# A fused hash-attention and gated-FFT kernel: whole-pair DMAs, transposes of two tokens of one head, bucket bits by DMA, weight split on GpSimd

## The chip, the cores and the metric

The kernel runs on one core of a Trainium2 chip. The metric is device time in microseconds (us): the median of several executions. Engines are called PE (TensorE matmul), VectorE or DVE, ScalarE or ACT, GpSimd or POOL, and SyncE or SP, which only issues DMAs here. A core has 16 DMA engines. Each engine works through its own instructions strictly in order. "Granted clock" is the TensorE clock that the throttle allowed, 1.0 being full speed.

## The reference, cut to what matters

Four batches, eight heads, 768 tokens, head size 64. Attention is masked by a hash: a query sees only the keys whose six projection signs ("bucket bits") equal its own. The result (512 wide) goes through three projections, a circular convolution of one of them along the tokens, a product of the three, and an output projection.

```python
q_bits = (np.einsum('bhsd,dk->bhsk', q, proj) > 0)       # proj: 64 x 6; k_bits likewise
mask = q_bucket[:, :, :, None] == k_bucket[:, :, None, :]
attn = softmax(where(mask, q @ k.T / 8, -1e9));  x = attn @ v        # per head
proj = x @ w_proj                                          # 512 -> 3 x 512: x1, x2, x3
x2_conv = irfft(rfft(x2) * rfft(filter))                   # along the 768 tokens
out = (x1 * x2_conv * x3) @ w_out
```

## The kernel before

The work goes by head pairs, 16 in all (four per batch). For a pair g the kernel loads q, k and v, transposes q and k on PE, copies them from PSUM to `tz` (DVE), casts them into the operands `row` (POOL), projects for the bits (`zps`, PE), and writes the bits beside q and k, so that one score matmul (`stp`) also carries the mask. ACT takes the exponential. `pv` multiplies with v; DVE makes T from it. Then the rows are normalised: the row sums travel to DRAM as reciprocals (`rdr`) and come back broadcast over partitions as R, and DVE multiplies: U = T * R. `xh` and `xl` are U split into two half-precision parts, the input of the projections (`x2`, `x`), which start when a batch's four pairs are done and run between the attention work of later pairs. The weights are split the same way once, early in the run.

The parts that matter (cuts marked `...`):

```python
def finish(g):                                   # end of a pair
    ...
    nc.vector.reciprocal(rl, rl)
    rdr = drp.tile([2, SEQ], FP32, ...)          # in DRAM; SEQ = 768
    nc.sync.dma_start(rdr.rearrange("h (p c) -> p h c", p=P), rl)
    R = nrm.tile([P, SEQ], FP32, tag="R", name="R", bufs=1)
    for par in range(2):                         # one DMA per head: 64 partitions each
        nc.sync.dma_start(
            R[HD * par : HD * par + HD, :], rdr[par : par + 1, :].to_broadcast([HD, SEQ])
        )
    ...
    nc.vector.scalar_tensor_tensor(              # U waits for R
        U, in0=T[:, 0:SEQ], scalar=vsd, op0=ALU.add, in1=R, op1=ALU.mult)
    nc.vector.tensor_copy(th, U)                 # xh
    nc.gpsimd.tensor_tensor(tl, U, th, ALU.subtract)   # xl

# loads of q and k: four DMAs each, runs of 256 bytes
for par in range(2):
    head = src[b, 2 * pr + par].rearrange("(c p j) d -> p c j d", c=3, p=P, j=2)
    ...
    for j in range(2):
        eng.dma_start(t_[:, :, j, par, :], head[:, :, j, :])

# bits: eight small DVE operations per pair
nc.vector.tensor_scalar(row[(which, par)][r0 : r0 + 6, cs], zs[hf][z0 : z0 + 6, :],
                        0.0, 0.5, ALU.is_gt, ALU.subtract)

# weight split, shared between DVE and POOL
nc.vector.tensor_copy(th, w32)
(nc.vector if c % 2 else nc.gpsimd).tensor_tensor(tl, w32, th, ALU.subtract)
```

The softmax here doesn't subtract the row's maximum and nothing guards it: scores larger than these inputs give would overflow.

## Time and profile before

| | before |
|---|---|
| time, median | 523.1 us (522.0 to 524.1) |
| PE busy / DVE / POOL | 469.4 / 322.5 / 156.1 us of 521.2 |
| projections start (first x2 matmul) | 113.7 us |
| first score matmul | 17.2 us |

The windows view of the kernel before, cut at the start of the projections: microseconds busy (instructions), granted clock, DMA share, GB/s.

```profile
core 0: us, PE busy (x) PEld busy (x) DVE busy (x) ACT busy (x) POOL busy (x), PEclk, DMA share, GB/s
0.00:113.70 113.70, 84.63 (x417) 40.99 (x418) 90.21 (x147) 61.62 (x81) 72.46 (x98) 0.91 0.63 162
113.70:521.20 407.50, 384.74 (x2137) 207.61 (x2135) 232.27 (x445) 168.20 (x241) 83.65 (x109) 0.99 0.19 53
```

PE's waits in the first 121 us of the kernel before (us in total, times, longest):

```profile
PE tps_q L198 <- DVE T L276: 6.6, 2, 5.2
PE tps_q L198 <- DMA nat_q<-in_q_dram: 4.6, 1, 4.6
...
PE hps L449 <- DVE pr_k_1_96 L232: 2.2, 1, 2.2
```

Apart from the first load, PE there waits for DVE's evacuations and bit writes.

### The profile page before, as it was taken

To read this page: it belongs to the slowest core of one execution; us is meant where nothing else is said; L and a number is where in the kernel's file an instruction comes from. 1 tells how busy PE (TensorE), PEld (TensorE's weight loads), DVE (VectorE), ACT (ScalarE), POOL (GpSimd) and SP (SyncE) were. 2 spreads that over 40 slices of the span, in tenths; PEclk is the share of its full clock that TensorE was granted. 3 is DMA by queue.
4 is the path that set the end of the run, shared out by engine and by line. 5 is a ranking of instruction groups with operands and counts; after the bars stand their busy time and mean duration, and the time that the engine had idled before them with its cause. 6 is when DMAs were issued, how large, how long until landed. Compare 5 with 4: busy or idle time off the path is not lost.

```text
span 521.2 us, 7013 instructions
## 1 busy us (share of the span) xinstructions
PE 469.4 (90%) x2552; PEld 248.6 (48%) x2552; DVE 322.5 (62%) x591; ACT 229.8 (44%) x321; POOL 156.1 (30%) x206
## 2 busy tenths in 40 slices
PE   4797657988998989999898998989999999999997
PEld 2343323544464545645354554645455556445553
DVE  4888987893756887353747878463645783036830
ACT  0496604883454553446365355336577310201102
POOL 4574993562414222232324131232311110000000
PEclk9898869998998999999999999999999999999999
DMA  9798514541313031324113040313010100300003
GB/s 215 186 287 218 171 32 102 123 121 34 91 32 91 1 93 32 93 91 139 45 32 91 14 109 1 93 44 120 20 32 1 33 30 1 121 1 1 0 2 121
DMA packets 82084, 39.93 MB, mean 77 GB/s; under 512 B 61953, under 2 KB 74753, under 8 KB 82049
## 3 DMA queue, kind: packets, MB, share of 16 engines
q1 hardware_dynamic: 78544, 38.62, 27.8%
q10 hardware_dynamic: 3504, 0.86, 0.8%
q8 instruction: 20, 0.33, 0.3%
q14 instruction: 16, 0.12, 0.1%
HBM read 32.97 MB, written 6.39 MB: 76 GB/s over the span
## 4 chain that ended last, share of the span: by engine, by line
PE 50%; DMA 17%; DVE 16%; issue 7%; POOL 5%; SPq 3%; ACT 2%; DVEq 0%; ACTq 0%; POOLq 0%
PE wout L488 8%; DMA R<-rdr 7%; PE pv L270 5%; DMA rdr<-rl 5%; PE stp L354 4%; PE x2b L488 3%; PE x2c L488 3%; PE zps L215 3%; PE x2a L488 2%; PE idrq L488 2%; DMA nat_v<-in_v_dram 2%; SPq L177 2%; PE fdft L488 2%; DVE U L304 1%; DMA flt_572<-in_moe_filter_fft_dram 1%
## 5 line engine op out<-in xcount | busy, mean ns | idle before, releaser
L276 DVE SCALAR_TENSOR_TENSOR T<-S,cst_sb,pv 64x512 f32<-64x512 f32 x64 | 38.9, 608 | 58.0 <-ACT S L275 57.3
L310 POOL TENSOR_TENSOR xl<-U,xh 128x768 f16<-128x768 f32 x16 | 26.5, 1654 | 97.0 <-DVE xh L308 97.0
L275 ACT COPY S<-pv 64x512 f32<-64x512 f32 x64 | 30.5, 477 | 46.1 <-PE pv L270 30.4
L215 PE MATMUL zps<-tz,projpad 128*38 128x384 f32 x128 | 29.0, 561 | 8.1 <-DVE tz L202 5.6
L198 PE MATMUL tps_q<-cst_sb,nat_q 128*128 128x128 f32 x96 | 24.9, 297 | 11.1 <-DVE T L276 6.6
L632 ACT ACTIVATE osb<-wout 128x512 f32<-128x512 f32 x24 | 14.3, 595 | 45.0 <-PE wout L488 44.9
L198 PE MATMUL tps_k<-cst_sb,nat_k 128*128 128x128 f32 x96 | 24.7, 288 | 7.7 <-DMA nat_k<-in_k_dram 2.5
L304 DVE SCALAR_TENSOR_TENSOR U<-T,vsd,R 128x768 f32<-128x768 f32 x16 | 16.5, 1032 | 23.5 <-DMA R<-rdr 20.5
L202 DVE TENSOR_SCALAR tz<-tps_q 128x384 f32<-128x384 f32 x32 | 17.6, 554 | 18.9 <-PE tps_q L198 18.4
L488 PEld LDWEIGHTS <-xh 128*128 128x128 f16 x192 | 18.9, 99 | 19.8 <-DVE xh L308 1.6
L198 PEld LDWEIGHTS tps_q<-cst_sb,nat_q 128*128 128x128 f32 x96 | 13.8, 151 | 20.4 <-DVE T L276 7.4
L359 ACT ACTIVATE pt_115<-stp,nmatch 128x768 f16<-128x768 f32 x16 | 14.5, 904 | 16.8 <-PE stp L354 16.6
L359 ACT ACTIVATE pt_111<-stp,nmatch 128x768 f16<-128x768 f32 x16 | 14.4, 901 | 15.5 <-PE stp L354 15.5
L198 PEld LDWEIGHTS tps_k<-cst_sb,nat_k 128*128 128x128 f32 x96 | 13.4, 147 | 16.4 <-issue 4.3
L359 ACT ACTIVATE pt_112<-stp,nmatch 128x768 f16<-128x768 f32 x16 | 14.4, 903 | 15.4 <-PE stp L354 15.2
L202 DVE TENSOR_SCALAR tz<-tps_k 128x384 f32<-128x384 f32 x32 | 17.5, 549 | 6.0 <-PE tps_k L198 4.0
L359 ACT ACTIVATE pt_106<-stp,nmatch 128x768 f16<-128x768 f32 x16 | 14.4, 902 | 14.9 <-PE stp L354 14.9
L359 ACT ACTIVATE pt_104<-stp,nmatch 128x768 f16<-128x768 f32 x16 | 14.4, 901 | 14.2 <-PE stp L354 7.3
L359 ACT ACTIVATE pt_110<-stp,nmatch 128x768 f16<-128x768 f32 x16 | 14.4, 902 | 11.8 <-PE pv L270 6.3
L354 PE MATMUL stp<-pr_q_0_87,pr_k_0_90 128*128 128x512 f16 x72 | 17.9, 325 | 1.6 <-ACT pt_108 L359 1.4
L354 PE MATMUL stp<-pr_q_0_86,pr_k_0_89 70*128 70x512 f16 x72 | 17.6, 333 | 1.7 <-ACT pt_104 L359 0.7
L488 PEld LDWEIGHTS <-wph_594 128*128 128x128 f16 x128 | 12.3, 98 | 13.8 <-issue 4.8
(1290 smaller groups left out, 1382.8 us busy)
## 6 DMA issues: line engine op xcount, KB each, us to landing
nat_q<-in_q_dram SPq DMA_DIRECT2D x64, 96.0 KB, 2.9
nat_v<-in_v_dram SPq DMA_DIRECT2D x32, 192.0 KB, 3.8
R<-rdr SPq DMA_DIRECT2D x32, 192.0 KB, 3.6
out_dram<-osb SPq DMA_DIRECT2D x24, 256.0 KB, 2.0
nat_k<-in_k_dram SPq DMA_DIRECT2D x56, 96.0 KB, 2.6
o_616<-in_moe_w_out_dram SPq DMA_DIRECT2D x1, 1024.0 KB, 7.5
nat_k<-in_k_dram ACTq DMA_DIRECT2D x8, 96.0 KB, 4.1
flt_572<-in_moe_filter_fft_dram SPq DMA_DIRECT2D x1, 768.0 KB, 7.1
```

Of the source, the lines that this page charges most:

```text
L198: nc.tensor.transpose(tps[:, ts(i, P)], nat[:, c3, j].rearrange("p h d -> p (h d)"), ident)
L202: nc.vector.tensor_scalar(tz[:, cs], tps, scl, None, ALU.mult)
L215: mm = nc.tensor.matmul(zps[64 * i : 64 * i + 38, :], projpad, tzs[i][:, cs])
L270: nc.tensor.matmul(pv, vpr[:, jt, :], pl[jt][:, lo_c:hi_c], start=(jt == 0), stop=(jt == NCH - 1),)
L275: nc.scalar.copy(S[rows, lo_c:hi_c], pv[HD:P, :])
L276: nc.vector.scalar_tensor_tensor(T[rows, lo_c:hi_c], in0=S[rows, lo_c:hi_c], scalar=mask[rows, :], op0=ALU.mult, in1=pv[0:HD, :], op1=ALU.add,
L304: nc.vector.scalar_tensor_tensor(U, in0=T[:, 0:SEQ], scalar=vsd, op0=ALU.add, in1=R, op1=ALU.mult)
L310: nc.gpsimd.tensor_tensor(tl, U, th, ALU.subtract)
L354: nc.tensor.matmul(stp[:, lo_c:hi_c], kp[kr, ts(jt, P)], qp[kr, lo_c:hi_c])
L359: nc.scalar.activation(pt[:, 0:SEQ], stp, AF.Exp, bias=nmatch, scale=LSCALE)
L488: nc.tensor.matmul(dest, lh, rh, start=(i == 0), stop=(i == len(terms) - 1))
L632: nc.scalar.mul(osb, po, 1.0 / YSCALE)
```

## The change

The intent: fewer and larger DMAs (q, k, v of a pair and R in one each, runs of 512 bytes), less DVE work (bits in two operations per pair and eight small DMAs; weight split on POOL). The transposed blocks now hold two tokens of one head instead of one token of two heads; the token order is carried through to the output. The core of the diff (cuts marked `...`; reorderings of v, of the convolution's output and of the stores, and the move of a few early loads to other DMA queues, are left out):

```diff
-    NPT = 12
+    NPT = 11
...
-        for par in range(2):
-            head = src[b, 2 * pr + par].rearrange("(c p j) d -> p c j d", c=3, p=P, j=2)
-            ... (one DMA for v, two for q and k, per head)
+        t_ = natp.tile([P, NCH, P], FP32, tag="nat", name=f"nat_{which}")
+        eng.dma_start(
+            t_,
+            src[b, 2 * pr : 2 * pr + 2].rearrange("h (c p j) d -> p (h c) (j d)", c=3, p=P, j=2),
+        )
...
-                for par, r0 in ((0, 64), (1, 0)):
-                    z0 = 64 * i + 32 * par
-                    nc.vector.tensor_scalar(
-                        row[(which, par)][r0 : r0 + 6, cs], zs[hf][z0 : z0 + 6, :],
-                        0.0, 0.5, ALU.is_gt, ALU.subtract,
-                    )
+            nc.vector.tensor_scalar(bt[:, par], zps, 0.0, 0.5, ALU.is_gt, ALU.subtract)
+            r0 = (64, 0)[par]
+            for i, which in enumerate(("q", "k")):
+                for j in range(2):
+                    z0 = HD * i + 6 * j
+                    nc.sync.dma_start(
+                        row[(which, par)][r0 : r0 + 6, HALF * j : HALF * j + HALF],
+                        bt[z0 : z0 + 6, par],
+                    )
...
-        for par in range(2):
-            nc.sync.dma_start(
-                R[HD * par : HD * par + HD, :], rdr[par : par + 1, :].to_broadcast([HD, SEQ])
-            )
+        rda = rdr[:, :]
+        nc.sync.dma_start(
+            R, bass.AP(tensor=rda.tensor, offset=rda.offset, ap=[[SEQ, 2], [0, HD], [1, SEQ]])
+        )
...
-            nc.vector.tensor_copy(th, w32)
+            nc.gpsimd.tensor_copy(th, w32)
...
-            (nc.vector if c % 2 else nc.gpsimd).tensor_tensor(tl, w32, th, ALU.subtract)
+            nc.gpsimd.tensor_tensor(tl, w32, th, ALU.subtract)
...
-            nc.vector.tensor_copy(th2, o32[:, c, :])
+            nc.gpsimd.tensor_copy(th2, o32[:, c, :])
```

More of the change, by code (lines that the diff above doesn't have):

```diff
@@ L134 @@
     cst_sb = cp.tile([P, P + 4], FP32, name="cst_sb")
-    nc.scalar.dma_start(cst_sb, cst_d.ap())
+    nc.scalar.dma_start(cst_sb[:, 0:P], cst_d.ap()[:, 0:P])
     ident = cst_sb[:, 0:P]
     mask = cst_sb[:, P : P + 1]
-    projpad = cp.tile([P, 38], FP32, name="projpad")
+    projpad = cp.tile([P, HD], FP32, name="projpad")
     nc.vector.memset(projpad, 0.0)
-    nc.scalar.dma_start(projpad[0:HD, 0:6], proj)
-    nc.scalar.dma_start(projpad[HD:P, 32:38], proj)
+    nc.gpsimd.dma_start(projpad[0:HD, 0:6], proj)
+    nc.gpsimd.dma_start(projpad[HD:P, 6:12], proj)
+    nc.gpsimd.dma_start(cst_sb[:, P : P + 4], cst_d.ap()[:, P : P + 4])
     nmatch = cp.tile([P, 1], FP32, name="nmatch")
@@ L167, in nat_load @@
     def nat_load(src, b, pr, which, eng):
-        shape = [P, 2, 3, 2, HD] if which == "v" else [P, 3, 2, 2, HD]
-        t_ = natp.tile(shape, FP32, tag="nat", name=f"nat_{which}")
-        for par in range(2):
-            head = src[b, 2 * pr + par].rearrange("(c p j) d -> p c j d", c=3, p=P, j=2)
-            if which == "v":
-                eng.dma_start(t_[:, par], head)
-            else:
-                for j in range(2):
-                    eng.dma_start(t_[:, :, j, par, :], head[:, :, j, :])
+        t_ = natp.tile([P, NCH, P], FP32, tag="nat", name=f"nat_{which}")
[3 more added lines that the diff above has]
+        )
         return t_
@@ L189, in prep_gen @@
         row = prs[g % NPR]
-        tzs = []
+        tz = {}
         for (which, scl), nat in zip((("q", QSCL), ("k", KSCL)), nats):
-            tz = tzp.tile([P, SEQ], FP32, tag=f"tz_{which}", name="tz")
-            for hf in range(2):
-                cs = slice(HALF * hf, HALF * hf + HALF)
+            for par in range(2):
                 tps = psW.tile([P, HALF], FP32, tag="w", name=f"tps_{which}")
-                for i in range(3):
-                    c3, j = divmod(3 * hf + i, 2)
-                    nc.tensor.transpose(
-                        tps[:, ts(i, P)], nat[:, c3, j].rearrange("p h d -> p (h d)"), ident
-                    )
-                    if i == 2:
-                        nc.vector.tensor_scalar(tz[:, cs], tps, scl, None, ALU.mult)
-                    yield 165
-            nc.gpsimd.tensor_copy(row[(which, 0)][0:HD, :], tz[0:HD, :])
-            nc.gpsimd.tensor_copy(row[(which, 1)][HD:P, :], tz[HD:P, :])
-            tzs.append(tz)
@@ L207, in prep_gen @@
-        last = None
-        zs = []
-        with tc.high_priority(offset=200):
-            for hf in range(2):
-                cs = slice(HALF * hf, HALF * hf + HALF)
-                zps = psW.tile([P, HALF], FP32, tag="w", name="zps")
-                zs.append(zps)
-                for i in (1, 0):
-                    mm = nc.tensor.matmul(
-                        zps[64 * i : 64 * i + 38, :], projpad, tzs[i][:, cs]
-                    )
-                    if last is not None:
-                        tc.add_manual_dep(
-                            mm.ins, last.ins.name,
-                            mybir.DependencyInfo(
-                                mybir.DependencyClass.NoSync, mybir.DependencyReason.DATA
-                            ),
-                            reason="column tiles side by side",
-                        )
-                    last = mm
@@ L227, in prep_gen @@
-        for hf in range(2):
-            cs = slice(HALF * hf, HALF * hf + HALF)
-            for i, which in enumerate(("q", "k")):
-                for par, r0 in ((0, 64), (1, 0)):
-                    z0 = 64 * i + 32 * par
-                    nc.vector.tensor_scalar(
-                        row[(which, par)][r0 : r0 + 6, cs], zs[hf][z0 : z0 + 6, :],
-                        0.0, 0.5, ALU.is_gt, ALU.subtract,
-                    )
-        yield 1700
-    def v_prep(g):
+                t_ = tzp.tile([P, HALF], FP32, tag=f"tz_{which}{par}", name="tz")
@@ new lines, in prep_gen @@
+                for c in range(3):
+                    nc.tensor.transpose(tps[:, ts(c, P)], nat[:, 3 * par + c, :], ident)
+                    if c == 2:
+                        nc.vector.tensor_scalar(t_, tps, scl, None, ALU.mult)
+                    yield 165
+                rows = slice(HD * par, HD * par + HD)
+                for j in range(2):
+                    nc.gpsimd.tensor_copy(
+                        row[(which, par)][rows, HALF * j : HALF * j + HALF],
+                        t_[HD * j : HD * j + HD, :],
+                    )
@@ new lines, in prep_gen @@
+                tz[(which, par)] = t_
+        for _ in range(4):
+            yield 160
+        last = None
+        bt = tzp.tile([P, 2, HALF], FP16, tag="bt", name="bt")
+        for par in range(2):
+            zps = psW.tile([P, HALF], FP32, tag="w", name="zps")
+            for i, which in ((1, "k"), (0, "q")):
+                mm = nc.tensor.matmul(zps[HD * i : HD * i + HD, :], projpad, tz[(which, par)])
+                if last is not None:
+                    tc.add_manual_dep(
+                        mm.ins, last.ins.name,
+                        mybir.DependencyInfo(
+                            mybir.DependencyClass.NoSync, mybir.DependencyReason.DATA
+                        ),
+                        reason="column tiles side by side",
+                    )
+                last = mm
+            nc.vector.tensor_scalar(bt[:, par], zps, 0.0, 0.5, ALU.is_gt, ALU.subtract)
+            r0 = (64, 0)[par]
+            for i, which in enumerate(("q", "k")):
+                for j in range(2):
+                    z0 = HD * i + 6 * j
+                    nc.sync.dma_start(
+                        row[(which, par)][r0 : r0 + 6, HALF * j : HALF * j + HALF],
+                        bt[z0 : z0 + 6, par],
+                    )
@@ L239, in v_prep @@
+        yield 700
+    def v_prep(g, eng=None):
         b, pr = divmod(g, NPAIR)
-        nat = nat_load(v, b, pr, "v", nc.sync)
+        nat = nat_load(v, b, pr, "v", eng or nc.sync)
         for par in range(2):
-            src = nat[:, par].rearrange("p c j d -> p (c j) d")
-            vpr = vts[g % 2][par]
-            nc.gpsimd.tensor_copy(vpr[:, :, 0:HD], src)
+            src = nat[:, 3 * par : 3 * par + 3, :].rearrange("p c (j d) -> p j c d", j=2)
+            vpr = vts[g % 2][par].rearrange("p (j c) d -> p j c d", j=2)
+            nc.gpsimd.tensor_copy(vpr[:, :, :, 0:HD], src)
@@ L245, in v_prep @@
             nc.gpsimd.tensor_tensor(
-                vpr[:, :, 64:96], src[:, :, 0:32], vpr[:, :, 0:32], ALU.subtract
+                vpr[:, :, :, 64:96], src[:, :, :, 0:32], vpr[:, :, :, 0:32], ALU.subtract
             )
             nc.gpsimd.tensor_tensor(
-                vpr[:, :, 97:P], src[:, :, 33:HD], vpr[:, :, 33:HD], ALU.subtract
+                vpr[:, :, :, 97:P], src[:, :, :, 33:HD], vpr[:, :, :, 33:HD], ALU.subtract
             )
@@ L332, in attn_gen @@
     def attn_gen():
-        nats = prep_loads(0, (nc.sync, nc.scalar))
-        prep0 = Feed(prep_gen(0, nats))
-        v_prep(0)
+        prep0 = Feed(prep_gen(0, prep_loads(0, (nc.sync, nc.sync))))
+        v_prep(0, nc.scalar)
+        late = prep_loads(1, (nc.sync, nc.sync))
         prep0.drain()
-        preps = [Feed(prep_gen(1, prep_loads(1, (nc.sync, nc.scalar))))]
+        preps = [Feed(prep_gen(1, late))]
         pv = Feed(iter(()))
@@ L514, in proj_gen @@
             ps = bank(DM, "x2a")
-            yield from group(ps, x2_terms(2 + j))
+            yield from group(ps, x2_terms(3 * j + 1))
             x1s = fbp.tile([P, DM], FP32, tag="xs", name="x1s")
@@ L519, in proj_gen @@
             ps = bank(DM, "x2b")
-            yield from group(ps, x2_terms(4 + j))
+            yield from group(ps, x2_terms(3 * j + 2))
             e_ = fbp.tile([P, DM], FP32, tag="e_", name="e_", bufs=1)
@@ L526, in proj_gen @@
             ps = bank(DM, "x2c")
-            yield from group(ps, x2_terms(j))
+            yield from group(ps, x2_terms(3 * j))
             s_, p_ = fold(ps, e_, j, fbp, 1)
@@ L588, in inv_gen @@
             cv = fbp.tile([P, SEQ], FP32, tag="cv", name="cv")
-            nc.vector.tensor_tensor(cv[:, 0:T3], asb, prq[:, 0:T3], ALU.add)
+            cvv = cv.rearrange("p (j c t) -> p c j t", j=2, c=3)
+            r_ = prq[:, 0:T3].rearrange("p (j t) -> p j t", j=2)
+            q_ = prq[:, T3 : 2 * T3].rearrange("p (j t) -> p j t", j=2)
+            a_ = asb.rearrange("p (j t) -> p j t", j=2)
+            nc.vector.tensor_tensor(cvv[:, 0], a_, r_, ALU.add)
             w_ = fbp.tile([P, T3], FP32, tag="w_", name="w_", bufs=1)
@@ L593, in inv_gen @@
             )
-            nc.vector.tensor_tensor(
-                cv[:, T3 : 2 * T3], w_, prq[:, T3 : 2 * T3], ALU.subtract
-            )
-            nc.vector.tensor_tensor(cv[:, 2 * T3 : SEQ], w_, prq[:, T3 : 2 * T3], ALU.add)
+            wv = w_.rearrange("p (j t) -> p j t", j=2)
+            nc.vector.tensor_tensor(cvv[:, 1], wv, q_, ALU.subtract)
+            nc.vector.tensor_tensor(cvv[:, 2], wv, q_, ALU.add)
             cvs[ct] = cv
@@ L632, in out_gen @@
             nc.scalar.mul(osb, po, 1.0 / YSCALE)
-            nc.sync.dma_start(ob[c // 2, c % 2], osb)
+            nc.sync.dma_start(ob[c % 3, c // 3], osb)
             yield 216
```

## The prediction

> **What bounds the kernel now.** The page's busy table: TensorE (PE) 469 of 521 us, VectorE (DVE) 322, GpSimd (POOL) 156. The windows view: from 121 us on PE is nearly full. In the first 117 us PE is busy only 88, DVE 93, over 80% in nearly every 13 us window; 30 of PE's 52 idle us lie there. The waits view names there: q/k loads at the start (4.6 + 2.5 us), then DVE results (T 8.5, tz 3.2, bit writes 4.4). From 52 to 78 us POOL is busy 25 of 26 us with the weight split, PE 16.4, and the granted clock falls to 0.82 and 0.66, some 4 us.
>
> **What the change does.**
> - Bits: eight DVE operations of 6x384 at 0.55 us per pair become two of 128x384, also 0.55 each (as tz's). DVE loses 3.3 us per pair, 53 in all, 26 in the first 121. In exchange eight small DMAs per pair: issue about 0.45 us each, landing about 2 (as lt's 2.1).
> - Loads: SyncE issues 15 DMAs per pair before and after: no relief. Runs grow from 256 to 512 B; the Trainium skill, "DMA: Bandwidth & Descriptors" (table at its top), puts line rate at 512 B. For 13 us engines are 95% busy: q, k should land earlier.
> - Weight split: DVE loses four 1536-column casts (5.3 us), two subtractions (3.5), four small casts (5.5): 14 us. POOL gains an estimated 17 (casts 1.7 each from 0.82 per 768 columns, subtractions 3.8, small casts 0.6).
> - POOL copies of q/k: twice as many of half width, 0.4 us more per pair. PE work unchanged.
>
> **On the critical path.** After 121 us nearly none; 2 to 5 us fewer gaps. Start: scores begin at 17.2 us, after eight bit writes in a row; I expect 13 to 14, gain 3 to 5 us. From 78 to 121 us: 3 to 5. From 26 to 78 us DVE stops being the limit, but POOL takes the whole split, 30 us of in-order work, and the weight tiles have two buffers, so SyncE's queue waits for POOL between weight loads, with other loads and bit DMAs behind: 3 to 9 us net, not the 14 that DVE sheds. Mutual slowing of DVE and POOL goes: the Trainium skill, "GPSIMD Engine Reference" (section 1, Specifications), says VectorE shares its SBUF interfaces; here a 512-column cast took 0.41 us once and 3.31 beside a long POOL operation.
>
> Sum: about 18 us. **Predicted 505 us, 80% range 493 to 518.** Chances: faster by over 2% 0.70, within 2% 0.27, slower by over 2% 0.03.
>
> **What would show each step.** Right: DVE total near 255 us, POOL near 180; PE within 5 us of 469; first scores before 15 us; DVE below 70% from 78 to 117 us; x2 beginning 12 us before today's 121, then the same 400 to within 5. Wrong: POOL solidly busy 40 to 85 us with PE waiting for transposes; SyncE waits on weight loads over 15 us; the span after x2's start shrinking by more than 10.
>
> **What would break it.** (1) POOL's long block stalls the tz buffers and with them PE's in-order queue: no gain before 80 us, total near 515. (2) Bit DMAs stuck on SyncE behind waits for lt or output tiles (150 and 122 us of waiting today) delay scores in the PE-bound part. (3) PE stays dense from the start and its clock loss vanishes: below 495.

## More of the kernel before

From the page of the kernel before: the span; busy time by engine; busy tenths of PE and DVE in 40 equal slices, with the granted clock in tenths; the group of the 16 U operations (busy, mean ns, idle time just before it and what ended it); and the issues of R (KB each, median us to landing).

```profile
span 521.2 us, 7013 instructions
...
PE 469.4 (90%) x2552; PEld 248.6 (48%) x2552; DVE 322.5 (62%) x591; ACT 229.8 (44%) x321; POOL 156.1 (30%) x206
...
PE   4797657988998989999898998989999999999997
...
DVE  4888987893756887353747878463645783036830
...
PEclk9898869998998999999999999999999999999999
...
L304 DVE SCALAR_TENSOR_TENSOR U<-T,vsd,R 128x768 f32<-128x768 f32 x16 | 16.5, 1032 | 23.5 <-DMA R<-rdr 20.5
...
R<-rdr SPq DMA_DIRECT2D x32, 192.0 KB, 3.6
```

PE has gaps in the first nine slices, where DVE is at 7 to 9 in all but the first; later PE is at 8 or 9 nearly everywhere. R lands 3.6 us after its issue and U waits for it 20.5 us in all, little over 1 us per pair.

PE is idle 29 us before the projections start and 23 us after.

## The result, and the profile after

The kernel after takes 639.3 us (638.2 to 639.6), the kernel before 523.6 us in the same rounds: ratio 1.221, 95% interval 1.217 to 1.225. A ratio here is always the mean time of one kernel's fast runs over that of the other's of the same rounds, so not quite the ratio of the medians quoted.

The page of the kernel after, same lines:

```profile
span 637.8 us, 7139 instructions
...
PE 494.5 (78%) x2552; PEld 262.0 (41%) x2552; DVE 266.7 (42%) x485; ACT 230.9 (36%) x321; POOL 177.2 (28%) x282
...
PE   5866724875695959779493969869598978999997
...
DVE  4354492342434537232232545633213266504760
...
PEclk9979775977896998979697998979798978999999
...
L298 DVE SCALAR_TENSOR_TENSOR U<-T,vsd,R 128x768 f32<-128x768 f32 x16 | 16.3, 1018 | 130.0 <-DMA R<-rdr 130.0
...
R<-rdr SPq DMA_DIRECT2D x16, 384.0 KB
```

DVE has lost 56 us of work, as intended, and is now busy in no slice above 7 tenths except for one 9 (the operation of 14.35 us below). Yet U waits 130.0 us for R, 8 us in each of the 16 pairs, where it waited 20.5. The difference, 109.5 us, is close to the 116 us that the kernel lost. PE's row is now full of dips, and so is the granted clock; PE's busy time rose by 25 us for the same 2,552 matmuls, at a mean clock of 0.887 instead of 0.974. The clock records in the trace show which comes first. Each of the 16 gaps between matmuls that is longer than 4.5 us overlaps a stretch at half clock; 15 of these gaps began 1.8 to 5.2 us before their stretch, the 16th fell into one that was running. Two stretches have no such gap beside them. All stretches together last some 143 us here and 27 us in the kernel before, where only one gap is that long. So beside the long gaps the clock sinks after the gap has opened, and does not open it; no run varied this by itself.

The windows view of the kernel after, again cut at the first x2 matmul:

```profile
0.00:140.80 140.80, 89.17 (x428) 45.79 (x429) 66.27 (x99) 64.39 (x83) 85.14 (x137) 0.82 0.45 133
140.80:637.80 497.00, 405.37 (x2126) 216.20 (x2123) 200.44 (x386) 166.54 (x239) 92.04 (x145) 0.91 0.14 44
```

Most of the loss, 90 us, lies after the projections have started, in the stretch that I had called PE-bound.

How a wait of DVE becomes one of PE, in the timeline of the kernel after (start, duration, operation; in brackets the idle time before it and what ended it):

```profile
199.94 1.02 DVE L298 SCALAR_TENSOR_TENSOR U<-T,vsd,R 128x768 f32<-128x768 f32 x1 [7.49 <-DMA R<-rdr]
200.88 0.68 DVE L563 TENSOR_TENSOR u__1591<-fdft,hB_672 128x512 f32<-128x512 f32 x1
...
201.61 0.48 PE L482 MATMUL x_1612<-xh,wph_595 128*128 128x384 f16 x1 [7.31 <-DVE u__1591 L563]
```

DVE stands 7.49 us with U at the head of its queue. Behind U waits u, which would empty a PSUM bank; PE stands 7.31 us because its next matmul needs that bank.

There is a second oddity in the same trace, seen in its timeline:

```profile
80.76 14.35 DVE L286 TENSOR_SCALAR rl<-lt 128x12 f32<-128x12 f32 x1 [0.65 <-DMA lt<-S]
...
94.54 0.53 POOL L242 TENSOR_TENSOR vt_1_132<-nat_v,vt_1_132 128x186 f16<-128x186 f32 x1
95.13 0.50 POOL L199 CAST pr_k_1_96<-tz 64x384 f16<-64x384 f32 x1
...
96.00 0.37 PE L264 MATMUL pv<-pt_113,vt_1_128 128*128 128x257 f16 x1 [12.61 <-DVE T L270]
```

A DVE operation on 12 elements per partition, which takes 0.17 us as a rule, is on record for 14.35 us. It ends at 95.11, in the gap of 0.06 us between two POOL operations; before that gap POOL had run weight and v operations back to back. PE pays 12.6 us.

**Why is R slow?** R is 128 rows of 3,072 bytes. I counted the DMA packets of that size in the trace's records; "at a time" is the sum of the packets' durations over the time from the first packet's start to the last one's end (medians over the 16 pairs).

```
kernel      packets per pair   first to last   at a time   one packet (median)
before      128                2.28 us         9.0         121 ns
after       128                8.31 us         2.0         121 ns
```

The packets are not slower; only two are in flight. The Trainium skill, page "DMA: Bandwidth & Descriptors", section "Why a DMA increments its semaphore by 16 and not by 1" (paragraph "How many engines (k)"), says that a DMA is spread over the largest number of engines, at most 16, that divides the slowest dimension of both access patterns. The new source pattern is `[[SEQ, 2], [0, HD], [1, SEQ]]`: its slowest dimension is 2. Before, each of the two DMAs had 64. For 2 the trace agrees: 2.0 packets at a time. For 64 the page gives 16 engines; 9.0 packets were in flight on average, so there the trace shows many engines, not their number.

### The profile page after: what moved, and what is told of

Its sections match the earlier page's. It is cut to its first block, busy times and chain, and to the rows that moved or that the text cites. A ratio compares the mean times of both kernels' runs of the same rounds, so it can differ in the third digit from the quotient of the medians.

```text
span 637.8 us, 7139 instructions
## 1 busy us (share of the span) xinstructions
PE 494.5 (78%) x2552; PEld 262.0 (41%) x2552; DVE 266.7 (42%) x485; ACT 230.9 (36%) x321; POOL 177.2 (28%) x282
## 4 chain that ended last, share of the span: by engine, by line
PE 46%; DMA 34%; DVE 9%; issue 5%; POOL 4%; SPq 1%; ACT 1%; DVEq 0%; ACTq 0%; POOLq 0%
DMA R<-rdr 23%; PE wout L482 5%; PE stp L348 5%; PE pv L264 5%; DMA rdr<-rl 5%; DVE rl L286 3%; PE x2b L482 2%; PE zps L211 2%; PE x2a L482 2%; PE x2c L482 2%; PE idrq L482 2%; DVE U L298 2%; PE fdft L482 2%; DMA nat_q<-in_q_dram 2%; DMA lt<-S 1%
## 5 line engine op out<-in xcount | busy, mean ns | idle before, releaser
L193 PE MATMUL tps_k<-cst_sb,nat_k 128*128 128x128 f32 x96 | 27.9, 326 | 36.5 <-DVE T L270 21.9
L193 PE MATMUL tps_q<-cst_sb,nat_q 128*128 128x128 f32 x96 | 26.5, 302 | 16.9 <-DMA nat_q<-in_q_dram 11.7
L193 PEld LDWEIGHTS tps_k<-cst_sb,nat_k 128*128 128x128 f32 x96 | 15.8, 170 | 47.9 <-DVE T L270 23.8
L353 ACT ACTIVATE pt_114<-stp,nmatch 128x768 f16<-128x768 f32 x17 | 15.3, 901 | 39.0 <-PE stp L348 38.8
L353 ACT ACTIVATE pt_106<-stp,nmatch 128x768 f16<-128x768 f32 x18 | 16.2, 900 | 34.5 <-PE stp L348 34.3
L211 PE MATMUL zps<-tz,projpad 128*64 128x384 f32 x128 | 26.4, 523 | 0.8 <-DVE tz L195 0.8
L353 ACT ACTIVATE pt_112<-stp,nmatch 128x768 f16<-128x768 f32 x17 | 15.3, 900 | 31.3 <-PE stp L348 31.1
L353 ACT ACTIVATE pt_105<-stp,nmatch 128x768 f16<-128x768 f32 x18 | 16.2, 900 | 27.9 <-PE stp L348 27.8
L221 DVE TENSOR_SCALAR bt<-zps 128x384 f16<-128x384 f32 x32 | 17.7, 555 | 18.2 <-PE zps L211 10.3
L353 ACT ACTIVATE pt_115<-stp,nmatch 128x768 f16<-128x768 f32 x17 | 15.3, 901 | 26.9 <-PE stp L348 26.6
L348 PE MATMUL stp<-pr_q_0_88,pr_k_0_91 128*128 128x512 f16 x72 | 20.6, 370 | 2.6 <-ACT pt_114 L353 0.8
L353 ACT ACTIVATE pt_113<-stp,nmatch 128x768 f16<-128x768 f32 x17 | 15.3, 901 | 18.4 <-PE stp L348 18.4
L353 ACT ACTIVATE pt_107<-stp,nmatch 128x768 f16<-128x768 f32 x18 | 16.2, 900 | 15.2 <-PE stp L348 14.9
```

The lines of the kernel that those rows point to most:

```text
L193: nc.tensor.transpose(tps[:, ts(c, P)], nat[:, 3 * par + c, :], ident)
L211: mm = nc.tensor.matmul(zps[HD * i : HD * i + HD, :], projpad, tz[(which, par)])
L348: nc.tensor.matmul(stp[:, lo_c:hi_c], kp[kr, ts(jt, P)], qp[kr, lo_c:hi_c])
L353: nc.scalar.activation(pt[:, 0:SEQ], stp, AF.Exp, bias=nmatch, scale=LSCALE)
```

## The experiments

Theory A: R's single DMA is carried by two engines; U then holds DVE's queue some 8 us per pair, and PE with it. Rival B: the eight bit DMAs on SyncE's queue and the weight split on POOL are what costs. Ratios are to the kernel before, on the same chip in the same rounds.

| run | what | median us | ratio (95% interval) | U's wait for R, us |
|---|---|---|---|---|
| before | | 523.1 | | 20.5 |
| after | | 639.3 | 1.221 (1.217 to 1.225) | 130.0 |
| e1 | after, R in two DMAs | 501.6 | 0.958 (0.954 to 0.963) | 13.3 |
| e2 | before, R in one DMA | 643.9 | 1.230 (1.224 to 1.237) | 125.4 |
| e3 | before, R in two DMAs, slowest dimension 2 | 642.9 | 1.229 (1.222 to 1.235) | 122.2 |
| e11 | the same, slowest dimension 4 | 587.5 | 1.130 (1.122 to 1.138) | 67.3 |
| e4 | e1, weight split as before | 506.1 | 0.968 (0.963 to 0.973) | 11.9 |
| e13 | after, weight split as before | 628.1 | 1.199 (1.191 to 1.207) | 123.0 |
| e5 | after, U emitted later | 631.7 | 1.207 (1.199 to 1.216) | 126.6 |
| e9, e12 | after, U forced later | 546.8, 546.6 | 1.049 (1.043 to 1.055), e12 one look | 40.4 (e12) |
| e6 | e1, U emitted later | 499.0 | 0.956 (0.950 to 0.962) | 11.3 |
| e10 | e1, U forced later | 496.4 | 0.953 (0.949 to 0.957) | 4.4 |
| e7 | e1, bits by DVE | 510.8 | 0.978 (0.972 to 0.983) | 31.6 |
| e8 | e1, loads in four DMAs each | 526.4 | 1.008 (1.001 to 1.014) | 21.1 |

All gave correct results.

### e1: R in two DMAs again, all else as in the kernel after

```diff
-        rda = rdr[:, :]
-        nc.sync.dma_start(R, bass.AP(..., ap=[[SEQ, 2], [0, HD], [1, SEQ]]))
+        for par in range(2):
+            nc.sync.dma_start(
+                R[HD * par : HD * par + HD, :], rdr[par : par + 1, :].to_broadcast([HD, SEQ])
+            )
```

> The kernel after, with R loaded by two DMAs of 64 rows as in the kernel before; nothing else undone. Theory A (R's single DMA has an outermost dimension of two and is carried by two DMA engines; VectorE's U then sits at the head of its queue for some 8 us per pair): U's wait for R falls from 130 us to about 20 to 30, R's 128 packets run again about 9 at a time, the granted clock returns above 0.95, and the time falls from 639 to 510 to 535 us. Rival B (the bit DMAs on SyncE's queue and the weight split on POOL are what costs): the time stays above 590 us.

Measured: 501.6 us, better than the theory's range. The windows view of e1, cut at its first x2 matmul, and its wait of U:

```profile
0.00:110.20 110.20, 86.90 (x429) 45.04 (x430) 56.25 (x99) 64.13 (x83) 87.87 (x138) 0.89 0.56 167
110.20:500.70 390.50, 378.08 (x2126) 206.44 (x2123) 202.51 (x386) 166.69 (x239) 95.16 (x145) 1.00 0.19 57
```

```profile
DVE U L298 <- DMA R<-rdr: 13.3, 10, 2.8
```

Undoing those lines alone returns 138 us; B falls. R's packets run 9.7 at a time again, 2.14 us from first to last, and the mean clock is 0.974. The rest of the change is a gain of 4.2%.

### e2, e3 and e11: only R is altered, in the kernel before

e2 puts the merged DMA into the kernel before:

> The kernel before, with only R's two DMAs merged into one as in the change. Theory A: 600 to 650 us, U waiting over 100 us for R, PE clock below 0.93. Rival B: under 545 us.

e3 and e11 keep two DMAs of 64 rows, and write the 64 rows as n x 64/n, with n = 2 and 4. Nothing else differs, neither bytes, rows nor issues:

```diff
-            R[HD * par : HD * par + HD, :], rdr[par : par + 1, :].to_broadcast([HD, SEQ])
+            R[HD * par : HD * par + HD, :],
+            bass.AP(tensor=rda.tensor, offset=rda.offset + SEQ * par, ap=[[0, n], [0, HD // n], [1, SEQ]]),
```

> The kernel before with R still in two DMAs of 64 rows, but each source pattern written as 2 x 32 rows, so that its outermost dimension is two. Theory A (count of engines follows the outermost dimension; both DMAs then share the same two engines): packets of 3,072 bytes run about 2 at a time, about 8 us from the first to the last of a pair, and the time is within 15 us of e2. Rival C (the cost comes from having one issue in place of two): the time is within 2% of 523 us. If the compiler merges the 2 x 32 back into 64, the packets will show about 9 at a time and the run says nothing.

> The kernel before with R in two DMAs whose source pattern is 4 x 16 rows. If the outermost dimension sets the number of engines: 3,072-byte packets about 4 at a time, 4 to 5 us from first to last, U's wait for R between 20 and 126 us, near 50 to 70 us, and the time 545 to 585 us, between the kernel before and e3.

Measured, with the packets counted as above:

```
kernel             first to last   at a time   U's wait   time
before (64, two)   2.28 us         9.0          20.5      523 us
e11    (4, two)    5.43 us         3.7          67.3      587.5
e3     (2, two)    9.31 us         2.0         122.2      642.9
e2     (2, one)    8.46 us         2.0         125.4      643.9
```

The waits of U in e2, e11 and e3, in this order:

```profile
DVE U L304 <- DMA R<-rdr: 125.4, 16, 12.0
```

```profile
DVE U L306 <- DMA R<-rdr: 67.3, 15, 7.3
```

```profile
DVE U L306 <- DMA R<-rdr: 122.2, 16, 9.3
```

The number in flight follows the slowest dimension, and not the number of issues: e3 has two issues and loses the same. Two DMAs with dimension 2 do not get four engines between them, they take turns on two. e11's time came out 2 us above its range, and its first to last at 5.43 us instead of 4 to 5. A microsecond more of U's waiting costs a little more than a microsecond of time (120 us for 102 from before to e3). Part of the excess is the clock: e2's 2,552 matmuls are busy 500.0 us, the kernel before's 469.4. That the granted clock sinks beside the gaps is on record, as said above; why it does was not tested. A single DMA with the 64 rows outermost could not be tried: it would have to step over partitions in its second dimension, which the check of the build refuses.

### e5, e6, e9, e10 and e12: is it the place of U in DVE's queue?

e5 issues U, xh and xl of a pair about one pair later in the program, R being slow as in the kernel after; e6 does it by half a pair, R in two DMAs.

```diff
+        pend.append((b, pr, T, R, vsd))      # end of finish(g)
...                                            # in pv_gen, after T of the next pair:
+                    if pend and par == 1 and lo_c == 0:    # e6: par == 0 and lo_c
+                        normalise()           # U, xh, xl of the pair before
```

> The kernel after, with R still in its one slow DMA, but U, xh and xl of a pair are issued about one pair later in VectorE's queue (at the first T of the next pair's second head), so that R has landed by then. Theory H (the 8 us more per pair cost so much because U waits at the head of VectorE's in-order queue and holds back the T and tz evacuations behind it, and through them PE): U's wait for R falls from 130 us to below 40 and the time to 505 to 540 us. Rival L (what counts is that the normalised x comes later for the projections): above 590 us.

> e1 (R in two DMAs, 501.6 us) with U, xh and xl issued about half a pair later in VectorE's queue. Theory H says that the 13 us of U's remaining wait for R are worth something too: wait below 4 us, time 490 to 500 us. Rival: PE is the limit there and nothing moves, within 3 us of e1.

In both U's wait missed its range. e5 gained 8 us, U still waited 126.6 us. e6 waited 11.3 us; its 499.0 us fit the theory's range and the rival's 3 us alike, so it decides nothing. The order of DVE's instructions in the build shows why (the numbers are places in DVE's queue); the kernel after, then e5, at one pair:

```
after: 194 U<-T,vsd,R   195 T<-S,cst_sb,pv 64x512   196 xh<-U   ...
e5:    194 T<-S,cst_sb,pv 64x512   195 U<-T,vsd,R   ...   197 xh<-U
```

The order that came out of the build had U back within one operation of its old place in 15 of the 16 pairs (in one it stood eight places later; e6 likewise left U within three places of that of e1 in all pairs but one). The edit had not made the kernel that I meant, so e5 says nothing about the theory. e9 (R slow) and e10 (R in two) add an ordering edge on DVE, without a semaphore, from T of the next pair to U:

```diff
+        if after is not None:
+            tc.add_manual_dep(u_op.ins, after.ins.name,
+                mybir.DependencyInfo(mybir.DependencyClass.NoSync, mybir.DependencyReason.DATA), ...)
```

In e9's trace this U stands ten places later, behind the first T of the next pair's second head.

> As e5, but with an ordering edge on VectorE that really puts U behind the first T of the next pair's second head (in e5 the build's ordering pass had moved U back to within one operation of its old place, so e5 tested nothing). R stays in its one slow DMA of some 10 us. Theory H (head of VectorE's in-order queue): U's wait for R falls from 130 us to below 40 us and the time to 505 to 540 us. Rival L (the later xh itself, or the two busy DMA engines, cost the time): above 590 us.

> e1 with the same kind of edge: U behind the last T of the next pair's first head, about half a pair later. Theory H: U's wait for R below 3 us (13 in e1), time 492 to 500 us. If PE is the limit: within 3 us of e1's 501.6 us.

e9: 546.8 us in three fast runs; its profiled run was a slow one of 817.8 us at a clock of 0.559 and is not read. e12 is the same kernel for another profile:

> The same kernel as e9, for a profile in the fast state (that of e9 fell in a run of 816 us at a granted clock of 0.56). Its fast runs were 547 us: 85 us better than e5, so theory H holds for most, but 45 us above e1. Expected in the trace, if H holds: U waits less than 40 us for R in all. For the rest, theory Q (loads and bit DMAs queued behind R's rows on the two engines that carry it): landing times of q and k loads issued within 8 us after R are 6 us or more longer than in e1, and PE's or POOL's waits for loads and bits exceed e1's by 20 us or more. Rival: U still waits, over 60 us.

e12 took 546.6 us at a clock of 0.94, as e9's fast runs. Its wait of U and its windows:

```profile
DVE U L306 <- DMA R<-rdr: 40.4, 7, 8.6
```

```profile
0.00:141.10 141.10, 90.33 (x429) 45.18 (x430) 66.03 (x99) 64.40 (x84) 85.12 (x137) 0.81 0.45 133
141.10:544.80 403.70, 380.56 (x2126) 207.61 (x2123) 202.72 (x386) 166.25 (x238) 90.31 (x145) 0.99 0.18 54
```

With R exactly as slow (2.0 packets at a time, 8.54 us), 92 us of the 138 us come back only because U stands later in the queue. So most of the cost is the head of DVE's queue and not R's latency as such, and rival L (above 590 us) falls; the time is still 7 us above the theory's range, and U's wait just misses its own (below 40 us). After the projections start, e12 needs 403.7 us where the kernel after needed 497.0 and e1 390.5. Of the 44 us of span that remain over e1, 31 lie before that start.

The records say where these 31 us come from. In the first four pairs the edge changes nothing: U stood behind that T in the kernel after already, and its places in DVE's queue are the same in both traces. So U still waits 31.0 of its 40.4 us in these four pairs, and 9.4 us in the other twelve together; the operation rl, which took 14.35 us in the kernel after, takes 14.23 here. Two comparisons in which one thing changes price the two: from e4 to e13 only R becomes one DMA, and the start of the projections moves from 112.2 to 129.0 us; from e13 to the kernel after only the weight split moves to POOL, and it moves on to 140.8 us. Theory Q is not needed for this part: before the start POOL waits 9.8 us for v (11.9 in e1), and of the waits for loads only PE's for q is longer (12.0 against 5.2 us). Over the whole run POOL waits 32.1 us for v, but the landing times that the theory spoke of are not resolved in these traces, so it is not shown.

e10: 496.4 us, within its range; U waits 4.4 us, where below 3 was expected. It is the fastest kernel, 4.7% under the kernel before. Its windows:

```profile
0.00:109.80 109.80, 85.54 (x428) 43.73 (x429) 55.84 (x99) 63.97 (x83) 87.70 (x138) 0.89 0.57 168
109.80:494.60 384.80, 376.67 (x2126) 206.84 (x2123) 201.35 (x386) 166.21 (x239) 100.19 (x145) 1.00 0.20 57
```

PE is busy 376.7 of the 384.8 us after the projections start: there 8 us are left. Against e1 the ratio interval overlaps (0.953 and 0.958 from different rounds), so the last 5 us are likely rather than shown.

### e4 and e13: the weight split back on DVE and POOL

e4 undoes the split in e1, e13 in the kernel after:

```diff
-            nc.gpsimd.tensor_copy(th, w32)
+            nc.vector.tensor_copy(th, w32)
-            nc.gpsimd.tensor_tensor(tl, w32, th, ALU.subtract)
+            (nc.vector if c % 2 else nc.gpsimd).tensor_tensor(tl, w32, th, ALU.subtract)
-            nc.gpsimd.tensor_copy(th2, o32[:, c, :])
+            nc.vector.tensor_copy(th2, o32[:, c, :])
```

> e1 with the weight split placed as in the kernel before (casts and every other subtraction on VectorE). In the kernel after, one VectorE operation of 128x12 (rl) took 14.35 us beside POOL's unbroken run of weight operations. Theory D (that stall is a second cost of the change): rl is at most 4 us, and the time is 5 to 12 us below e1. Rival (the split is hidden): within 4 us of e1, either way.

> The kernel after with only the weight split put back as in the kernel before; R stays in its one DMA. In the kernel after (and in e12) one VectorE operation of 128x12 (rl) took 14.3 us while POOL ran weight operations without a gap. Theory D (the split on POOL starved VectorE there and costs some of the 116 us): rl's longest below 4 us and the time 622 to 632 us, 7 to 17 below 639. Rival (the stall falls where PE had nothing else to do, or the VectorE work given back costs as much): 634 to 646 us.

e4: 506.1 us, 4.5 us slower than e1, so theory D failed there: with R repaired rl's longest is 1.4 us in e1 anyway, and moving the split to POOL is a small gain. e13: 628.1 us, 11 us faster than the kernel after, and the first x2 matmul comes at 129.0 instead of 140.8 us; D holds there. rl in e13 (duration in ns, min/median/max):

```profile
L286 DVE TENSOR_SCALAR rl<-lt x16: 160/173/1121, 48.9 to 507.3; 128x12 f32<-128x12 f32 x16
```

So the split had a share of about 11 us in the loss, but only in company with the slow R, which shifted rl into POOL's unbroken run. That POOL's run is what held rl is an inference from the end of rl in POOL's gap and from its vanishing with the run; no run isolates the two engines. The Trainium skill, page "GPSIMD Engine Reference", section "Specifications", says that POOL shares its SBUF interfaces with VectorE, with contention for VectorE operations in a two-port mode or with two SBUF inputs. rl has one tensor input, and no run here shows its mode, so whether the page's case is this one stays open.

### e7 and e8: where the other 4% come from

e7 is e1 with the bits written by eight DVE operations as before; e8 is e1 with the q, k and v loads cut into four DMAs each with runs of 256 bytes.

```diff
 e7:
-            nc.vector.tensor_scalar(bt[:, par], zps, 0.0, 0.5, ALU.is_gt, ALU.subtract)
...
-                    nc.sync.dma_start(row[...][r0 : r0 + 6, ...], bt[z0 : z0 + 6, par])
+                    nc.vector.tensor_scalar(row[...][r0 : r0 + 6, ...], zps[z0 : z0 + 6, :],
+                                            0.0, 0.5, ALU.is_gt, ALU.subtract)
 e8:
-        eng.dma_start(t_, src[b, 2 * pr : 2 * pr + 2].rearrange("h (c p j) d -> p (h c) (j d)", ...))
+        for par in range(2):
+            for j in range(2):
+                eng.dma_start(t_[:, 3 * par : 3 * par + 3, HD * j : HD * j + HD], head[:, :, j, :])
```

> e1 with the bits written by eight VectorE operations of 6x384 per pair as in the kernel before, no bit DMAs; layout, loads and weight split stay as in the change. If the bit change is what brings the gain of e1 over the kernel before (21 us): VectorE's busy time rises from 259 to about 312 us and the time to 510 to 520 us. If the gain comes from the loads or from elsewhere: 498 to 506 us.

> e1 with the q, k and v loads of a pair each cut into four DMAs with runs of 256 bytes, the layout in SBUF and all else unchanged (24 SyncE DMAs per pair rather than 16). If load size matters: start of the scores later by 1 to 3 us and the time 505 to 515 us. If loads are hidden after the start: within 4 us of e1.

e7: 510.8 us; DVE is busy 308.8 us instead of 258.8. The bits are worth some 9 us (ratios 0.978 and 0.958). With the 4.5 us of the split (e4) that leaves, if the pieces add up, some 7 of e1's 21 us that no run assigns. e8: 526.4 us, far over the range: 25 us lost. Of the 22.4 us between the spans of the profiled runs, 19.2 lie before the projections, whose start moves from 110.2 to 129.4 us; the scores do not start later (14.8 against 15.1 us). In the timelines of SyncE, e1 first, then e8, the first FFT table is issued so:

```profile
2.51 1.60 SPq L391 DMA_DIRECT2D f0h<-f0h  x1
```

```profile
55.41 0.48 SPq L393 DMA_DIRECT2D f0h<-f0h  x1
```

With 25 instead of 16 issues per pair (the expectation miscounted by one) of about 0.4 to 0.7 us each, SyncE issues almost without a gap from 14 to 60 us, and the tables, the filter and the weights come after that. e8 also let the build choose another order, so it shows that the count of issues can cost this much in the early part, but not how much of it is order, and nothing about 256 against 512 bytes by itself.

## Why the prediction was right or wrong, point by point

It forecast 505 us (493 to 518) and the kernel takes 639.3. **The step that failed** is the item "Loads: SyncE issues 15 DMAs per pair before and after: no relief". The merging of R's two DMAs entered only there, as one issue less in the count of 15; its transfer was never priced, and no term of the sum stands for it. The term should have read: the merged R has a slowest dimension of 2, is carried by 2 engines, needs about 8 us from first to last instead of 2.3, and U's wait grows from 20.5 to 130 us. I cited the DMA page's table at its top and did not use the paragraph on the number of engines on the same page. The second half of the error was to treat a wait behind a full PE as free: "After 121 us nearly none". U stands at the head of DVE's in-order queue, and the evacuations behind it are what PE needs next (e9).

Point by point:

- "Sum: about 18 us", 505 us: that is what the rest of the change does, 501.6 us in e1. But the pieces were wrong and cancelled, so that this agreement is luck. Before the projections start I expected 9 to 19 us and e1 gained 3.5 (113.7 to 110.2); after it I expected 2 to 5 and e1 gained 17 (407.5 to 390.5), PE's idle time there falling from 23 to 12 us. "The same 400 to within 5" failed, and so did "x2 beginning 12 us before": moreover I had taken 121 us for its start from the chain of waits, which lists only long pieces; the first x2 matmul is at 113.7.
- DVE near 255, POOL near 180, PE within 5 us of 469: 266.7, 177.2 and 494.5 in the kernel after; 258.8, 183.0 and 465.0 in e1. Right once R is repaired; the kernel after's extra PE time is the lower clock.
- First scores before 15 us: 15.1 us, from 17.2. Slightly missed. "q, k should land earlier" held for k only: q's transposes start at 5.1 us instead of 4.6, k's at 7.8 instead of 8.3. The three transposes of one head now wait for the DMA of the whole pair. No run separates runs of 512 bytes from runs of 256, so what the DMA page says of them is neither confirmed nor denied here.
- DVE below 70% from 78 to 117 us: 24.0 of 39 us in the kernel after, 14.35 of them the one operation rl; 21.5 in e1. Right.
- The warning of POOL's long block: real in the kernel after (11 us in e13), and a small gain without the slow R (e4). SyncE's waits at the weight loads were 17 us in the kernel after, over the 15 that I had named as a bad sign.
- "Mutual slowing of DVE and POOL goes": wrong in the kernel after, where one operation of DVE stood 14.35 us.
- Bit DMAs that delay scores: PE waited 2.7 us for them in the kernel after and 1.5 in e1. This fear did not come true.
- The chance of 0.03 for slower by over 2%: far too small for a bundle of edits of which one had not been priced.

What remains open: what exactly held rl for 14.35 us, and the 13 us that e12 needs beyond e1 after the projections start.

## What to carry to other kernels

Before merging DMAs, write down the slowest dimension of both access patterns of the merged one: a leading dimension of two heads gives it two of sixteen engines, and halving the issues made the transfer 3.6 times as long (8.31 against 2.28 us). A wait at the head of an in-order engine delays whatever stands behind it, even when that engine is half idle: place the consumer of a long transfer where the transfer has surely landed, and check in the built order that it really stands there. When a bundle of edits loses, undo the edits one at a time: here two lines hid a gain of 4%, and a later placed U probably adds to it (496.4 us).

## What the Trainium skill lacked or had wrong

- "DMA: Bandwidth & Descriptors", section "Rules for kernel authors", advises against two transfers to disjoint partition halves, and for one transfer of 128 partitions in their place. For R's broadcast from two DRAM rows that advice made the kernel 23% slower (e2, 643.9 against 523 us), because the merged source has a slowest dimension of 2. Another row of the same table names the rule that forbids it; the two rows should refer to each other.
- The same page states how many engines a DMA gets, and the runs agree where the number is small (3.7 packets at a time with 4, 2.0 with 2). What it does not say outright is that two such DMAs in flight then share these few engines; e3's two took 9.31 us together, no less than one merged (8.46 us in e2).
- The same page puts the sequencer's dispatch at about 50 ns, but in its account of DMAs issued from GpSimd; for an issue from SyncE it gives no figure. Here SyncE's issues take 0.33 to 0.56 us (medians by kind), those of the six-partition bit DMAs 0.66 us, and 25 per pair filled its queue (e8).
- No page says that a VectorE operation can stand through a whole run of separate POOL operations. Here one that takes 0.17 us as a rule stood 14.35 us during such a run and ended in a gap of 0.06 us; the cause is inferred.
